# A new order of steps in the opening and at the passage into the loop of an attention and FFN kernel

## The chip, the cores and the metric

The kernel runs on one core of a Trainium2 chip. The metric is the device time of one execution in microseconds (us), the median of several runs. The engines are PE (TensorE, matmuls), DVE (VectorE), ACT (ScalarE), POOL (GpSimd) and SP, which only issues transfers. Each engine works through its own instructions in program order and waits for the others by semaphores.

## The reference

```python
# q, k, v: (8, 8, 576, 64): batch, heads, sequence, head size
k_p = k.reshape(B, H, 72, 8, D).mean(axis=3)          # 8 neighbours pooled: 72 keys
v_p = v.reshape(B, H, 72, 8, D).mean(axis=3)
attn = softmax(q @ k_p.T / sqrt(D)); x = attn @ v_p    # -> x: (8, 576, 512)
xn = (x - mean) / sqrt(var + 1e-6) * g_ln              # per token
out = x + relu(xn @ w_ch1) @ w_ch2                     # 512 -> 2048 -> 512
```

## The kernel before

There are 36 tiles of 128 tokens, in nine chunks c of four tiles. For exactness in float32 each large matmul is three float16 matmuls on high and low parts. Chunks 0 and 1 use the weights as they are; from chunk 2 on the two FFN matmuls go by a scheme of seven products of half-sized blocks in place of eight (as Strassen's), for which sums of blocks of W1 and W2 are made on the way.

The kernel's work is written as small generators, named steps. Each `yield` ends a part. Two strings, START (chunks 0 and 1 and all preparation) and STEADY (the loop over chunks 2 to 8, with what is left of chunk 2's weights and of its second matmul), list step names; `run` goes through a string and advances the named step by one part. So the order of names is the program order on every engine, written out by hand; nothing reorders it except at the seam between the two strings, where the first parts of STEADY that are ready are moved forward. A name's n-th occurrence is its n-th part: the issue of matmuls is one part, the evacuation of their result on ACT or DVE another.

The steps that the text names:

- HK.b.i, HV.b.i: half of the keys or values of batch b: an SP load into one of two buffers (kr, vr), then pooling of 8 neighbours on POOL (L647 to L673) or DVE (L651, L668). HK fills the block kblk, HV ends with a maximum and a split into high and low parts; D spreads the values to their places by DMA.
- A.t: scores of tile t: matmuls (L787), maximum and subtraction on DVE (L797, L802), exponential on ACT, the low part on POOL (L823), and a transposing DMA on SP's queue (L834). B.t: attention values (L926, L927), then scaling and statistics on DVE (L934 to L955), z on POOL or DVE.
- R, C, S, M1, M2: raw weight load, conversion and maximum (C: L523 a maximum, L539 a conversion, both DVE), split into high and low (L486 on DVE), and the scale from the maximum (M1, M2: L558, L559, L443, L444 on DVE around one PE transpose L466).
- F.c.f: one tile of the first FFN matmul, 12 matmuls (L1110), relu on ACT (L1119), low part on DVE (L1121). In chunk 0 a third index takes half the columns. G.c.tt.half: half of the second FFN matmul of tile tt, 24 matmuls of 512 columns (L1313), then one DVE instruction that adds it to x (L1324).
- P.c.h.f.m: one of the seven products m, 6 matmuls of 256 columns (L1154), then an ACT copy (L1173) or a DVE addition (L1168, L1171). WH joins the products of an f into the hidden tile (L1184). TW: sums of W2's blocks (DVE L1233, POOL L1238 to L1246). TS.c: token scales of a chunk, a chain of DVE instructions on 128x4 elements (L1028 to L1059). EL, ER, ES, EP: left factors of the second matmul's products.

What couples them are buffers. PSUM in the opening: one buffer for A, one for B, three for F and G, one for the rest. In the loop: one for A and B together, six for P and G; the products 1, 6 and 7 of a block share a bank, so do 2 and 4, and 5 and 3, and each such bank is used again only after its evacuation. A step's matmuls that need a bank stand on PE until the step that had it is evacuated.

Of the kernel before, what the change touches and what calls it, by code (L numbers as in the profile page):

```python
# [87 lines left out]
F.0.12 S.2.4 S.2.4 S.2.5 B.6 HV.2.1 HV.2.1 F.0.15 S.2.5 S.2.5 S.2.6 F.0.14 F.0.15 B.6 B.6 B.6 A.10 A.11 A.10 F.0.13
F.0.13 S.2.6 S.2.6 S.2.7 HV.2.1 HV.2.1 F.0.14 F.0.14 F.0.15 F.0.15 S.2.7 S.2.7 G.0.0.1 G.0.1.1 G.0.2.1 HV.2.1 HV.2.1
HV.2.1 HV.2.1 B.7 B.7 A.10 HV.3.0 HV.3.0 HV.3.0 HV.3.0 G.0.0.1 T.1.0 T.1.0 B.7 HV.3.0 HK.3.0 HK.3.0 G.0.0.1 G.0.0.1  # L90
HV.3.0 A.10 A.10 HV.3.1 B.7 B.7 G.0.1.1 G.0.1.1 G.0.1.1 HV.3.0 HV.3.0 B.8 B.9 G.0.3.1 A.11 A.11 G.0.2.1 HV.3.1 HV.3.1
HK.3.1 G.0.2.1 G.0.2.1 B.9 V.10 F.1.0 F.1.1 F.1.0 A.11 HV.3.1 HV.3.1 A.11 A.11 G.0.3.1 F.1.2 T.1.0 HV.3.1 HV.3.1
# [1367 lines left out]
```

## Time and profile before

| | us |
|---|---|
| median of 3 runs (lowest, highest) | 813.83 (812.39 to 814.22) |
| the profiled execution, its own time | 812.09 |
| its span, first to last instruction | 810.3 |
| PE busy in the span | 780.9 |
| DVE busy in the span | 666.6 |

The profile is of one execution. Its span is what the engines' rows cover; the execution's own time is 1.8 us longer. PE's busy time is 96% of the span, with the granted clock at its full level. Times in the rows are counted from the start of the span.

### The profile page before, as it was taken

Reading aid. Unit: us, or ns where it says so; the run is one execution under the profiler, and the core shown is the slowest. Engines: PE = TensorE matmul, PEld = TensorE weight load, DVE = VectorE, ACT = ScalarE, POOL = GpSimd, SP = SyncE. Lnnn points to the kernel's source line nnn. Section 1 sums busy time; section 2 is a strip of 40 time slices with the busy share of each in tenths; the row PEclk is TensorE's granted clock in tenths of the full one; section 3 lists DMA queues with packets and bytes.
Section 4 is the critical chain, followed back from the end, with each engine's and each line's share of the span. In section 5 each row is a group of like instructions: output and inputs, shape, how many; then the busy total and the mean of one; then the engine's idle time right before and its main releaser. Section 6 shows DMA issues by size and latency. Waiting matters only on the chain.

```text
span 810.3 us, 17383 instructions
## 1 busy us (share of the span) xinstructions
PE 780.9 (96%) x6618; PEld 608.3 (75%) x6618; DVE 666.6 (82%) x1352; ACT 470.5 (58%) x880; POOL 488.8 (60%) x601
## 2 busy tenths in 40 slices
...
GB/s 355 283 167 301 236 168 126 205 18 8 45 114 121 181 208 132 199 187 243 199 176 177 222 188 238 131 260 161 233 99 209 162 131 167 169 153 161 77 120 130
DMA packets 181507, 138.91 MB, mean 171 GB/s; under 512 B 143792, under 2 KB 151600, under 8 KB 179248
## 3 DMA queue, kind: packets, MB, share of 16 engines
...
## 4 chain that ended last, share of the span: by engine, by line
PE 55%; DVE 6%; ACT 1%; issue 1%; DVEq 0%; ACTq 0%
PE ps_f L1271 25%; PE ps_f L1154 25%; PE ps_a L787 2%; DVE w L1192 1%; PE ps_f L1313 1%; PE ps_a L926 1%; PE ps_a L927 1%; DVE ring L1184 1%; DVE x L1288 0%; DVE phl L1168 0%; DVE raw L1168 0%; DVE mx L797 0%; DVE raw L1012 0%; DVE raw L1013 0%; DVE y L1043 0%
## 5 line engine op out<-in xcount | busy, mean ns | idle before, releaser
L1271 PE MATMUL ps_f<-ring,w 128*128 128x256 f16 x2016 | 231.3, 273 | 1.3 <-DVE w L1192 1.0
L1271 PEld LDWEIGHTS <-w 128*128 128x128 f16 x2016 | 196.6, 98 | 25.2 <-DVE w L1192 1.5
L1154 PE MATMUL ps_f<-zts,w 128*128 128x256 f16 x1680 | 206.8, 273 | 2.5 <-DVE x L1324 1.2
L1154 PEld LDWEIGHTS <-w 128*128 128x128 f16 x1680 | 163.5, 98 | 23.4 <-issue 3.9
L1313 PE MATMUL ps_f<-w,ring 128*128 128x512 f16 x576 | 126.4, 379 | 2.3 <-DVE x L1324 2.2
L1173 ACT COPY raw<-ps_f 128x256 f32<-128x256 f32 x160 | 56.3, 372 | 91.4 <-PE ps_f L1154 80.7
L1313 PEld LDWEIGHTS <-ring 128*128 128x128 f16 x576 | 56.1, 98 | 68.3 <-issue 2.6
L1154 PE MATMUL ps_f<-zts,tsp 128*128 128x256 f16 x672 | 91.0, 272 | 1.7 <-ACT raw L1173 1.7
L1110 PE MATMUL ps_f<-zts,w 128*128 128x512 f16 (+1 forms) x480 | 85.9, 336 | 2.5 <-DVE ring L1121 0.9
L1190 ACT CAST w<-w 128x512 f16<-128x512 f32 x96 | 59.0, 618 | 44.1 <-POOL w L1210 21.5
L1192 POOL TENSOR_TENSOR w<-w 128x512 f16<-128x512 f32 x48 | 58.4, 1216 | 32.1 <-ACT w L1190 22.6
L1110 PEld LDWEIGHTS <-w 128*128 128x128 f16 x480 | 46.4, 98 | 39.0 <-issue 3.3
L1154 PEld LDWEIGHTS <-tsp 128*128 128x128 f16 x672 | 65.0, 98 | 10.1 <-issue 2.3
L823 POOL TENSOR_TENSOR phl<-e,phl 128x512 f16<-128x512 f32 x32 | 40.9, 1278 | 45.6 <-ACT phl L813 45.6
L1209 POOL TENSOR_TENSOR w<-raw 128x256 f32<-128x256 f32 x32 | 24.8, 775 | 65.8 <-ACT raw L1201 38.1
L1288 DVE SCALAR_TENSOR_TENSOR x<-ps_f,y,x 128x256 f32<-128x256 f32 (+1 forms) x84 | 42.0, 517 | 23.7 <-PE ps_f L1271 22.5
L1079 POOL TENSOR_TENSOR hl<-raw,hl 128x640 f16<-128x640 f32 x28 | 40.9, 1463 | 24.9 <-ACT hl L1077 24.7
L1288 DVE SCALAR_TENSOR_TENSOR x<-ps_f,cy,x 128x256 f32<-128x256 f32 (+1 forms) x84 | 42.1, 516 | 13.1 <-PE ps_f L1271 12.5
L1192 DVE TENSOR_TENSOR w<-raw,w 128x512 f16<-128x512 f32 (+1 forms) x64 | 44.9, 708 | 3.9 <-ACT w L1190 3.8
L1168 DVE TENSOR_TENSOR raw<-ps_f,raw 128x256 f32<-128x256 f32 x80 | 32.2, 415 | 15.7 <-ACT raw L1173 9.2
L787 PE MATMUL ps_a<-kblk,q 128*128 128x144 f32 (+1 forms) x320 | 42.0, 289 | 1.4 <-PE ps_f L1154 0.8
L1119 ACT ACTIVATE ring<-ps_f 128x512 f16<-128x512 f32 (+1 forms) x40 | 19.4, 506 | 38.4 <-PE ps_f L1110 38.4
...
## 6 DMA issues: line engine op xcount, KB each, us to landing
...
```

Of the source, the lines that this page charges most:

```text
L787: nc.tensor.matmul(ps[r, p // 2, p % 2 * 2 * KV : (p % 2 + 1) * 2 * KV], lhsT=q[:, p, r], rhs=kblk[b % NKB][:, p, :], start=True, stop=True,)
L823: nc.gpsimd.tensor_tensor(out=ph[:, 0, :, KA:P], in0=e[:, :, 0:KA], in1=ph[:, 0, :, 0:KA], op=ALU.subtract)
L1079: nc.gpsimd.tensor_tensor(out=zhl[:, 1, :], in0=src, in1=zhl[:, 0, :], op=ALU.subtract)
L1110: nc.tensor.matmul(ps, lhsT=w[:, part, fs], rhs=zT[:, kz, cols], start=(n == 0), stop=(n == 3 * NKT - 1),)
L1154: nc.tensor.matmul(ps, lhsT=w[:, part, f * P : (f + 1) * P], rhs=z, start=m in (1, 2, 4, 5) and n == 0, stop=m in (2, 3, 4, 7) and n == 3 ...
L1168: nc.vector.tensor_tensor(out=o, in0=ps, in1=o, op=ALU.add)
L1173: nc.scalar.copy(out=o, in_=ps)
L1190: nc.scalar.copy(out=hi, in_=src)
L1192: engine.tensor_tensor(out=lo, in0=src, in1=hi, op=ALU.subtract)
L1271: nc.tensor.matmul(ps, lhsT=wt[2][:, left, part, f * HC + u * P : f * HC + (u + 1) * P], rhs=b[:, f // FPB, wp, f % FPB], start=n < 4 and ...
L1288: nc.vector.scalar_tensor_tensor(out=x, in0=ps, scalar=scale, in1=x, op0=ALU.mult, op1=ALU.add)
L1313: nc.tensor.matmul(ps, lhsT=h[:, part, i, cols], rhs=w[:, wp, j], start=(n == 0), stop=(n == 3 * NFT // 2 - 1),)
```

## The change

Both strings get a new order in one stretch each: START from its sixth line to its end (60 to 160 us of the profile, on PE), and STEADY from its first step to about the first products of chunk 3's second half (240 to 375 us), and a handful of exchanges of neighbours later. No code changes: the same steps, the same number of instructions on each engine, the same buffers. The core of the diff, without the lines that the text does not speak of:

```diff
--- before.py
+++ after.py
@@ START @@
...
-F.0.5.1 A.6 C.1.5 C.1.5 S.2.1 F.0.3.1 F.0.4.1 A.6 C.1.6 S.2.1 S.2.1 S.2.2 F.0.5.1 F.0.3.1 F.0.3.1 F.0.4.1 F.0.4.1 C.1.4
-C.1.4 C.1.7 A.6 S.2.2 S.2.2 S.2.3 HK.2.0 HK.2.0 S.2.3 S.2.3 HV.2.0 HV.2.0 HK.2.1 A.7 A.7 F.0.6.1 B.4 F.0.7.1 F.0.6.1
-C.1.6 F.0.7.1 A.7 A.7 M1.1 F.0.5.1 F.0.5.1 B.4 C.1.4 C.1.4 C.1.5 C.1.5 F.0.6.1 F.0.6.1 C.1.6 C.1.6 HV.2.0 B.4 A.7
-HK.2.1 HK.2.1 R.2.4 R.2.4 A.6 A.6 HV.2.0 R.2.5 R.2.5 R.2.6 R.2.6 HK.2.1 HK.2.1 HV.2.0 HV.2.0 A.8 A.8 M1.1 G.0.0.0 B.5
-G.0.1.0 A.7 A.7 M1.1 M1.1 S.1.4 C.2.4 B.5 B.6 F.0.7.1 F.0.7.1 G.0.2.0 S.1.4 S.1.4 S.1.5 C.1.7 C.2.5 G.0.0.0 G.0.0.0
-G.0.3.0 S.1.5 S.1.5 S.1.6 B.4 C.1.7 C.1.7 R.2.7 R.2.7 HV.2.1 A.8 A.8 C.2.6 S.1.6 S.1.6 S.1.7 B.6 G.0.1.0 G.0.1.0 A.8
-B.4 HV.2.0 HV.2.0 B.5 HV.2.1 HV.2.1 A.8 A.8 HV.2.1 HV.2.1 A.9 B.4 B.4 HK.3.0 A.9 B.7 A.9 A.9 S.1.7 S.1.7 F.0.8 F.0.8
-C.2.7 G.0.2.0 G.0.2.0 C.2.4 C.2.4 C.2.4 B.5 G.0.3.0 G.0.3.0 C.2.5 C.2.5 C.2.5 C.2.6 C.2.6 C.2.6 F.0.8 F.0.8 C.2.7 B.7
-HV.2.1 HV.2.1 HV.3.0 B.5 B.5 B.5 HV.2.1 B.6 A.9 A.9 A.9 A.10 A.10 F.0.9 F.0.10 F.0.11 B.8 F.0.9 F.0.10 F.0.11 C.2.7
...
+HV.1.1 HV.1.1 D.1 D.1 R.1.7 R.1.7 B.4 HK.2.0 S.2.1 S.2.1 S.2.2 C.1.6 F.0.4.1 F.0.4.1 F.0.3.1 F.0.3.1 F.0.6.1 F.0.7.1
+F.0.7.1 F.0.5.1 A.6 B.4 S.2.2 S.2.2 S.2.3 F.0.6.1 A.7 C.1.5 F.0.5.1 F.0.5.1 B.4 B.4 C.1.5 C.1.7 C.1.7 S.2.3 S.2.3
+HV.2.0 HV.2.0 A.5 A.5 HK.2.0 A.6 A.6 HK.2.1 R.2.4 R.2.4 B.5 A.7 B.5 M1.1 F.0.6.1 F.0.6.1 C.1.5 C.1.5 F.0.7.1 F.0.7.1
+HK.2.0 HK.2.0 A.7 HK.2.1 HK.2.1 R.2.5 R.2.5 A.7 A.7 HK.2.1 HK.2.1 HV.2.0 HV.2.0 B.4 B.5 HV.2.0 HV.2.0 A.8 A.8 G.0.0.0
+B.6 M1.1 G.0.1.0 G.0.2.0 M1.1 M1.1 S.1.4 C.2.4 C.1.6 G.0.0.0 G.0.0.0 S.1.4 S.1.4 S.1.5 C.2.5 A.8 S.1.5 S.1.5 C.1.6
+C.1.6 S.1.6 R.2.6 R.2.6 C.1.7 C.1.7 R.2.7 R.2.7 B.4 B.4 HV.2.1 HK.3.0 S.1.6 S.1.6 S.1.7 A.8 B.5 C.2.6 G.0.1.0 G.0.1.0
+C.2.4 S.1.7 S.1.7 G.0.2.0 G.0.2.0 A.8 B.6 HV.2.0 HV.2.0 B.5 HV.2.1 HV.2.1 B.6 HV.2.1 HV.2.1 B.5 B.5 HV.2.1 HV.2.1 A.8
+A.8 HV.3.0 A.9 A.9 G.0.3.0 F.0.8 F.0.9 B.7 F.0.8 C.2.7 F.0.9 G.0.3.0 G.0.3.0 F.0.10 F.0.8 F.0.8 F.0.11 C.2.5 C.2.5
+C.2.5 F.0.10 C.2.6 C.2.6 C.2.6 C.2.7 C.2.7 C.2.7 C.2.4 C.2.4 F.0.11 F.0.9 F.0.9 F.0.12 F.0.12 A.9 A.9 F.0.10 F.0.10
+M2.1 HK.3.0 A.9 A.9 A.9 A.10 A.10 M2.1 F.0.13 M2.1 M2.1 S.2.4 F.0.11 F.0.11 F.0.14 F.0.12 F.0.12 F.0.15 S.2.4 S.2.4
+S.2.5 F.0.14 F.0.13 B.6 HV.2.1 B.7 B.8 S.2.5 S.2.5 S.2.6 F.0.15 B.6 HV.2.1 HV.2.1 F.0.13 F.0.13 S.2.6 S.2.6 S.2.7
...
@@ STEADY @@
-P.2.0.0.2 P.2.0.0.1 P.2.0.0.5 P.2.0.1.2 P.2.0.0.1 P.2.0.0.1 P.2.0.0.6 P.2.0.1.1 P.2.0.1.1 P.2.0.1.1 P.2.0.0.5 P.2.0.0.5
-P.2.0.0.6 P.2.0.0.6 HV.4.0 KW.1.1 KW.1.1 A.12 A.12 P.2.0.1.6 TW.0.0.0 TW.0.0.0 P.2.0.0.2 P.2.0.0.2 P.2.0.0.4 P.2.0.1.5
-P.2.0.0.7 P.2.0.0.3 TW.0.0.0 TW.0.0.0 P.2.0.1.6 P.2.0.1.6 P.2.0.1.7 TW.0.0.1 TW.0.0.1 TW.0.0.1 TW.0.0.1 P.2.0.0.4
-P.2.0.0.4 TW.0.0.0 A.12 A.12 HV.4.0 HV.4.0 TW.0.0.0 TW.0.0.0 TW.0.0.1 P.2.0.1.2 P.2.0.1.2 P.2.0.1.4 P.2.0.2.2 P.2.0.1.4
-P.2.0.1.4 P.2.0.1.5 P.2.0.1.5 P.2.0.0.7 P.2.0.0.7 P.2.0.3.1 P.2.0.1.3 TW.0.1.0 A.12 P.2.0.0.3 P.2.0.0.3 P.2.0.3.5
-P.2.0.2.1 WH.2.0.0 TW.0.1.0 TW.0.1.1 P.2.0.1.7 P.2.0.1.7 TW.0.1.0 WH.2.0.0 WH.2.0.0 TW.0.1.1 P.2.0.1.3 P.2.0.1.3
...
-P.2.1.3.6 P.2.1.3.6 P.2.1.2.2 P.2.1.2.2 P.2.1.2.4 B.15 A.16 P.2.1.2.7 P.2.1.3.7 TS.3 B.15 HV.4.1 HV.4.1 TW.1.0.0 Z.14.0
-Z.14.0 TW.1.0.1 TW.1.0.0 TW.1.0.0 P.2.1.2.4 P.2.1.2.4 Z.14.1 Z.14.1 TW.1.0.1 TW.1.0.1 TW.1.0.0 P.2.1.3.3 P.2.1.3.3
-P.2.1.3.2 P.2.1.3.2 P.2.1.3.4 P.2.1.3.4 P.2.1.3.4 P.2.1.2.3 P.2.1.2.3 TW.1.0.1 A.16 P.2.1.2.7 P.2.1.2.7 WH.2.1.2 B.15
-P.2.1.3.7 P.2.1.3.7 WH.2.1.3 A.16 WH.2.1.2 WH.2.1.2 TW.1.1.0 TW.1.1.0 TS.3 WH.2.1.3 WH.2.1.3 A.16 B.15 B.15 TW.1.1.0
-TS.3 TW.1.1.1 TS.3 TS.3 TS.3 HV.5.0 HV.5.0 KW.1.0 KW.1.0 TW.1.0.0 TW.1.0.0 A.17 KW.0.1 KW.0.1 XT.14.0 XT.14.0 XT.14.1
-XT.14.1 TW.1.0.1 TW.1.0.1 A.16 A.16 A.17 G.2.0.1 P.3.0.1.2 P.3.0.0.2 G.2.3.1 P.3.0.0.1 P.3.0.1.1 TW.1.1.0 Z.15.0 HV.4.1
-HV.4.1 Z.15.1 P.3.0.1.1 P.3.0.1.1 P.3.0.0.1 P.3.0.0.1 TW.1.1.0 Z.15.0 Z.15.0 TW.1.1.1 Z.15.1 Z.15.1 HV.5.0 HV.5.0
-XT.15.0 XT.15.0 TW.1.1.0 TW.1.1.0 G.2.0.1 G.2.2.1 G.2.0.1 G.2.0.1 TW.1.1.1 TW.1.1.1 P.3.0.0.2 P.3.0.0.2 TW.1.2.0
-TW.1.2.0 A.17 A.17 P.3.0.1.2 P.3.0.1.2 P.3.0.1.4 B.16 P.3.0.0.4 TW.1.2.0 TW.1.2.0 P.3.0.1.4 P.3.0.1.4 G.2.1.1 TW.1.1.1
-TW.1.2.1 TW.1.2.1 G.2.2.1 A.17 TW.1.2.0 TW.1.2.1 TW.1.3.0 TW.1.3.0 TW.1.3.0 B.16 HV.5.0 HV.5.0 TW.1.1.1 TW.1.1.1
...
+P.2.0.1.2 P.2.0.0.1 P.2.0.1.1 P.2.0.1.1 P.2.0.1.1 HV.4.0 KW.1.1 KW.1.1 A.12 A.12 P.2.0.0.2 P.2.0.0.5 P.2.0.0.1
+P.2.0.0.1 TW.0.0.0 TW.0.0.1 TW.0.0.1 A.12 TW.0.0.1 TW.0.0.1 P.2.0.0.5 P.2.0.0.5 TW.0.0.0 P.2.0.1.2 P.2.0.1.2 P.2.0.1.4
+P.2.0.0.6 P.2.0.0.3 P.2.0.1.6 TW.0.0.0 TW.0.0.0 P.2.0.0.6 P.2.0.0.6 A.12 P.2.0.1.6 P.2.0.1.6 P.2.0.1.4 P.2.0.1.4 HV.4.0
+HV.4.0 TW.0.0.1 TW.0.0.0 TW.0.0.0 TW.0.0.0 P.2.0.0.3 P.2.0.0.3 HV.4.0 HV.4.0 A.13 TW.0.1.0 P.2.0.0.2 P.2.0.0.2
+P.2.0.0.4 P.2.0.1.5 P.2.0.0.7 P.2.0.1.7 P.2.0.0.4 P.2.0.0.4 P.2.0.1.5 P.2.0.1.5 P.2.0.1.3 P.2.0.3.2 A.12 A.12 A.12
+TW.0.1.1 P.2.0.0.7 P.2.0.0.7 P.2.0.3.1 WH.2.0.0 TW.0.1.0 P.2.0.1.7 P.2.0.1.7 P.2.0.2.2 A.13 P.2.0.3.5 P.2.0.2.1
...
+P.2.1.2.4 A.16 B.15 B.15 P.2.1.2.6 P.2.1.2.6 P.2.1.2.4 P.2.1.2.4 P.2.1.3.5 P.2.1.3.5 P.2.1.3.2 P.2.1.3.2 P.2.1.3.4
+P.2.1.2.7 P.2.1.3.3 P.2.1.3.4 P.2.1.3.4 TW.1.0.1 B.15 B.15 TW.1.1.0 P.2.1.2.3 P.2.1.2.3 P.3.0.0.2 P.2.1.2.7 P.2.1.2.7
+WH.2.1.2 TW.1.1.0 P.2.1.3.7 P.2.1.3.7 P.2.1.3.3 P.2.1.3.3 WH.2.1.3 TW.1.0.1 A.16 TW.1.0.1 WH.2.1.2 WH.2.1.2 WH.2.1.3
+WH.2.1.3 G.2.3.1 TS.3 TS.3 TS.3 TS.3 TS.3 TS.3 HV.5.0 HV.5.0 KW.1.0 KW.1.0 TW.1.0.0 TW.1.0.0 A.17 KW.0.1 KW.0.1 XT.14.0
+XT.14.0 XT.14.1 XT.14.1 A.17 G.2.0.1 P.3.0.0.1 P.3.0.1.2 G.2.2.1 Z.15.0 TW.1.0.1 Z.15.1 A.16 Z.15.0 Z.15.0 TW.1.1.0
+TW.1.1.0 TW.1.0.1 TW.1.0.1 TW.1.0.1 A.16 A.16 A.16 TW.1.1.0 Z.15.1 Z.15.1 TW.1.1.1 TW.1.1.1 G.2.0.1 TW.1.1.1 TW.1.1.1
+P.3.0.0.1 P.3.0.0.1 TW.1.2.0 HV.5.0 HV.5.0 XT.15.0 XT.15.0 TW.1.1.0 TW.1.1.0 G.2.0.1 G.2.0.1 TW.1.2.0 TW.1.1.1 A.17
+A.17 P.3.0.0.2 P.3.0.0.2 P.3.0.0.4 B.16 P.3.0.0.4 P.3.0.0.4 TW.1.2.0 TW.1.2.0 TW.1.2.1 G.2.3.1 TW.1.2.1 HV.5.0 HV.5.0
+TW.1.1.1 TW.1.1.1 XT.15.1 XT.15.1 P.3.0.0.6 P.3.0.1.1 P.3.0.0.5 P.3.0.0.6 P.3.0.0.6 P.3.0.1.1 P.3.0.1.1 P.3.0.0.7
+P.3.0.1.6 P.3.0.1.6 P.3.0.1.6 A.17 TW.1.2.0 TW.1.2.0 TW.1.2.0 A.18 A.17 A.17 B.16 P.3.0.1.2 P.3.0.1.2 P.3.0.1.4 G.2.1.1
...
```

In the opening the scores A.6, A.7 and A.9 and the values B.4 to B.6 come earlier among the F and G steps, the conversions C.1.4 earlier and C.1.7 later, M1.1 behind G.0.0.0, A.10 and B.8 later. In the passage the products begin in another order, TS.3 goes in one piece behind WH.2.1.3 and G.2.3.1, and the four second halves of G.2 come in the order 3, 0, 2, 1 instead of 0, 3, 2, 1.

## Rows read from the trace of the kernel before

**Rows 1.** The page's span, and the busy time of each engine: us, share of the span, instructions.

```profile
span 810.3 us, 17383 instructions
...
PE 780.9 (96%) x6618; PEld 608.3 (75%) x6618; DVE 666.6 (82%) x1352; ACT 470.5 (58%) x880; POOL 488.8 (60%) x601
```

**Rows 2.** Busy time of each engine by stretches: stretch, its length, then us busy (and instructions) on each engine, PE's granted clock, the share of the DMA engines that was busy, GB/s.

```profile
60.00:150.00 90.00, 84.11 (x558) 47.87 (x557) 82.48 (x156) 63.33 (x88) 69.05 (x83) 1.00 0.77 211
150.00:240.00 90.00, 89.16 (x443) 40.94 (x442) 67.33 (x115) 23.89 (x42) 41.51 (x39) 1.00 0.24 64
240.00:285.00 45.00, 43.67 (x400) 34.44 (x399) 40.24 (x80) 25.82 (x55) 29.92 (x44) 1.00 0.67 146
285.00:325.00 40.00, 36.40 (x240) 22.68 (x239) 38.19 (x91) 18.77 (x35) 23.46 (x33) 1.00 0.74 168
325.00:340.00 15.00, 14.56 (x98) 8.53 (x98) 10.46 (x22) 4.92 (x10) 12.15 (x20) 1.00 0.89 196
340.00:380.00 40.00, 40.00 (x390) 36.12 (x389) 36.23 (x79) 29.60 (x60) 30.33 (x39) 1.00 0.82 221
```

**Rows 3.** PE's timeline in the opening: start, duration, what ran and how often without a break, and in brackets the idle time ahead of it and what ended it.

```profile
74.66 1.47 PE L1110 MATMUL ps_f<-zts,w 128*128 128x256 f16 x12 [0.61 <-DVE ring L1121]
...
81.54 0.23 PE L466 MATMUL ps_m<-ident,rowmax 128*128 128x128 bf16 x1 [1.51 <-DVE rowmax L444]
81.87 5.34 PE L1313 MATMUL ps_f<-w,ring 128*128 128x512 f16 x24
...
87.73 5.34 PE L1313 MATMUL ps_f<-w,ring 128*128 128x512 f16 x24
...
107.28 2.54 PE L1110 MATMUL ps_f<-zts,w 128*128 128x512 f16 x11 [0.81 <-DVE x L1324]
110.51 0.39 PE L1110 MATMUL ps_f<-zts,w 128*128 128x512 f16 x1 [0.70 <-DVE w L486]
...
120.48 1.89 PE L1110 MATMUL ps_f<-zts,w 128*128 128x512 f16 x8 [0.31 <-DVE ring L1121]
```

**Rows 4.** PE's timeline in the passage, the same columns.

```profile
239.60 2.78 PE L1154 MATMUL ps_f<-zts,w 128*128 128x256 f16 x24 [0.84 <-DVE x L1324]
...
255.52 0.49 PE L1154 MATMUL ps_f<-zts,tsp 128*128 128x256 f16 x3 [1.09 <-ACT raw L1173]
...
309.01 1.22 PE L787 MATMUL ps_a<-kblk,q 128*128 128x144 f32 x8 [0.81 <-PE ps_f L1154]
310.07 5.34 PE L1313 MATMUL ps_f<-w,ring 128*128 128x512 f16 x24
315.25 1.47 PE L1154 MATMUL ps_f<-zts,w 128*128 128x256 f16 x12
316.56 5.34 PE L1313 MATMUL ps_f<-w,ring 128*128 128x512 f16 x24
...
325.44 5.34 PE L1313 MATMUL ps_f<-w,ring 128*128 128x512 f16 x24 [2.22 <-DVE x L1324]
...
337.62 0.49 PE L1154 MATMUL ps_f<-zts,tsp 128*128 128x256 f16 x3
```

**Rows 5.** DVE's timeline in the opening, the same columns.

```profile
78.63 1.33 DVE L558 TENSOR_SCALAR wm<-wm 128x4 f32<-128x4 f32 x1
...
89.61 0.21 DVE L934 TENSOR_SCALAR sm<-ps_a,cv 128x8 f32<-128x8 f32 x1
...
91.65 0.39 DVE L1121 SCALAR_TENSOR_TENSOR ring<-ps_f,ring 128x256 f16<-128x256 f32 x1
...
119.77 0.66 DVE L1121 SCALAR_TENSOR_TENSOR ring<-ps_f,ring 128x512 f16<-128x512 f32 x1
```

**Rows 6.** DVE's groups in 60 to 100 us by line and shape: count, busy us, mean ns of one, idle time ahead.

```profile
L523 DVE TENSOR_REDUCE wm<-raw 128x1 f32<-128x1024 f32 x2 | 2.4, 1212 | 0.0
...
L802 DVE TENSOR_TENSOR e<-ps_a,mx 128x576 f32<-128x576 f32 x3 | 2.3, 758 | 0.3
L797 DVE TENSOR_REDUCE mx<-ps_a 128x8 f32<-128x576 f32 x3 | 2.2, 745 | 0.0
...
L539 DVE SCALAR_TENSOR_TENSOR w<-w,tsp 128x1024 int32<-128x1024 int32 x1 | 1.2, 1208 | 0.0
```

**Rows 7.** POOL's timeline in the opening, and one row of it at 346 us.

```profile
77.79 2.15 POOL L483 TENSOR_TENSOR w<-w 128x1024 f16<-128x1024 f32 x1 [1.09 <-ACT w L481]
...
84.55 1.71 POOL L671 TENSOR_TENSOR vr<-vr 72x256 f32<-72x256 f32 x1
...
87.73 1.25 POOL L673 TENSOR_TENSOR vp<-vr 72x64 f32<-72x64 f32 x1
...
98.23 0.72 POOL L655 TENSOR_TENSOR kblk<-kr 64x72 f32<-64x72 f32 x2
...
346.16 1.61 POOL L1246 TENSOR_TENSOR phl<-kr,phl 128x512 f16<-128x512 f32 x1
```

**Rows 8.** DVE's timeline in the passage.

```profile
241.56 0.42 DVE L1168 TENSOR_TENSOR raw<-ps_f,raw 128x256 f32<-128x256 f32 x1 [2.01 <-ACT raw L1173]
...
253.74 0.67 DVE L668 TENSOR_REDUCE vp<-vr 72x64 f32<-72x512 f32 x1
...
318.43 1.11 DVE L1042 TENSOR_TENSOR a<-a,ve 128x4 f32<-128x4 f32 x1
...
324.63 0.75 DVE L1324 SCALAR_TENSOR_TENSOR x<-ps_f,cy,x 128x512 f32<-128x512 f32 x1
```

216 lines of the change are left out of this document (107 added, 109 removed).

## The prediction, made before the changed kernel ran

> **What bounds the kernel now.** I read the busy shares first: PE 780.9 of 810.3 us, DVE 666.6 [rows 1]. PE's clock is 1.00 in every stretch [rows 2], so the matmuls themselves can't get shorter; a new order can only change PE's idle time. The windows say where that lies [rows 2]: 5.89 us of it in 60 to 150, 0.84 in 150 to 240, 1.33 in 240 to 285, 3.60 in 285 to 325, 0.44 in 325 to 340, none in 340 to 380. The change reaches 61 to 160 and 240 to 375, nearly the same places.
>
> PE's timeline names the waits. In the opening there are 0.61 on an evacuation (L1121), 1.51 on the row maximum of W1's second half (L444), 0.81 ahead of F.0.8 (L1324) and 0.70 inside it (L486), 0.31 at F.0.12 [rows 3]. In the passage there are 1.09 on an ACT copy, 0.81 ahead of A.17's scores, 2.22 ahead of G.2.2.1 [rows 4]. Most of them are DVE being late, and DVE is busy for 82.48 of 90 us in the opening and 38.19 of 40 in 285 to 325 [rows 2]: there it is a second bound, close under PE.
>
> The idle column understates a wait. The 24 matmuls of a G step take 5.18 us from start to start (310.07 to 315.25), 0.216 each, and the 12 of two P steps 1.31 (315.25 to 316.56), 0.655 a P step [rows 4]; a lone matmul ahead of a change of step is drawn with 0.39 [rows 3], so a wait costs its idle time and about 0.16. With 5.89 + 5.37 us of idle time and some 15 waits the ceiling of any gain is near 13.7 us; the waits that stay or come new take most of it.
>
> **The change part by part.** No instruction is added, removed or resized. All costs are positions.
>
> *Opening, up to G.0.1.0.* G.0.0.0 needs the bank of F.0.5.1, so it starts when DVE has evacuated that: 81.87 now [rows 3]. Ahead of that evacuation DVE loses a maximum of W1 (C.1.7, 1.21 [rows 6]) and M1.1's chain, from 78.63 [rows 5] to the transpose at 81.54 [rows 3], 2.8 us, and gains B.4's finish (as B.5's, 89.61 to 91.65, 2.04 [rows 5]) and one C.1.4 conversion (1.21 as L539 [rows 6]). Net 0.8 less, and none to 0.7 of small waits besides: I take 0.9, G.0.0.0 at 81.0. B.5's matmuls (0.68, 87.05 to 87.73 [rows 3], the first by G's 5.18) are already done by then, where before they stand behind G.0.0.0. The 1.51 wait is not merely moved: M1.1's transpose now stands behind G.0.0.0 and B.6, by when DVE has long passed the row maximum. G.0.1.0 then starts near 81.0 + 5.18 + 0.68 (B.6) = 86.9, with B.6 done, against 87.73 with B.6 and a wait (0.9 together) to come: 1.7 gained.
>
> *Opening, G.0.2.0 to F.0.12.* After two G steps PE reaches A.9 at 97.3; A.9 needs A.8's maximum and subtraction done (0.4 wait, from DVE's new order) and the K block from POOL. A step of scores takes 1.06 (309.01 to 310.07 [rows 4]), so G.0.3.0 ends at 103.9. F.0.8 no longer follows B.7, and the weights it waits for (L486) stand two places earlier on DVE: the 0.81 and 0.70 go. PE alone would start F.0.12 at 103.9 + 4 x 2.59 (12 matmuls of 0.216 each) + 0.68 = 114.9. DVE allows less: F.0.12 needs F.0.9's evacuation, which starts at 119.77 [rows 5], less A.9's maximum and subtraction (0.75 + 0.76 [rows 6]) and B.7's finish (2.04), which now come behind it: 116.2, or down to 114.2 if DVE's own small waits go too. F.0.12 thus starts between 114.9 and 116.9. Before, it starts at 120.48 [rows 3] with A.10 (1.0) and B.8 (0.7) done that now come later, so the like time is 118.8. Gain 1.9 to 3.9.
>
> The 3.5 us of DVE work pushed behind F.0.9 must be hidden later. Cover: DVE has 7.5 us free in 60 to 150 and 22.7 in 150 to 240, where PE is almost full [rows 2]. Without that cover all 3.5 would come back, at A.10 and B.8. I take 3.3 for the opening (the 0.31 at F.0.12 and the waits after it can go too); ends 1.5 and 5.2. POOL and SP: HK.2.0's second half goes behind HV.2.0's 4.4 us of pooling (84.55 to 88.98 [rows 7]), which frees a K buffer at about 91 instead of 82. Behind the load that waits for it, SP's queue has R.2.5, the transpose of A.7, loads of V and the last raw weights, which land some 7 us later than before; their readers (C.2.6, C.2.7) stand ahead of F.0.9's evacuation, 13 us on. Cost nothing; were they 1 us late, 1 us.
>
> 150 to 240 is full on PE with DVE at 67.33 of 90 [rows 2]: a gain of the opening arrives at 239.6 whole.
>
> *Passage, early part.* PE's P steps begin in the order 0.1.2, 0.0.1, 0.1.1, A.12 instead of 0.0.2, 0.0.1, 0.0.5, 0.1.2 (all of chunk 2). This makes two new waits. P.2.0.1.4 uses the bank of P.2.0.1.2, whose evacuation DVE issues behind A.12's 1.5 us: A.12's scores end at 239.6 + 3 x 0.655 + 1.0 = 242.6, the evacuation 2 us later, PE is there at 243.9: 0.8. P.2.0.0.4 uses that of P.2.0.0.2, now evacuated behind P.2.0.0.3, a reduction of V (0.67) and a sum of W2 of like size, six places later, where it was the first of all at 241.56 [rows 8]: PE is there at 247.3, the evacuation is done at 248.9: 1.6. Further 0 to 0.8 at G.2.3.0, and 0.5 in small waits. The 1.09 at 255.52 [rows 4] goes. G.2.0.0 starts 1 to 2.1 us later than before.
>
> *Passage, late part.* G.2.2.1 waits 2.22 us [rows 4] for the bank of G.2.0.1, whose evacuation stands on DVE behind TS.3, token scales of 128x4 elements with 1.11 us on a single instruction, and starts at 324.63 [rows 8]. In the new order the first step of TS.3 comes eleven places later, G.2.3.1 and G.2.0.1 are exchanged, A.17 comes behind the first of them, and G.2.2.1's bank is one that P steps have long freed. All idle time of 285 to 340 (4.04 [rows 2], four waits, 4.7 us with 0.16 each) can go; one of 0.45 comes at P.3.0.0.2. Followed through PE's new order from the later G.2.0.0, G.2.1.1 ends at 337.35 to 338.5, against 337.62 [rows 4], with four more P steps (2.62) done: 1.75 to 2.9 gained. I take 1.8; ends 0.5 and 3.
>
> *A rule against it.* Row first: L558 works on four columns and takes 1.33 us, to 79.96 [rows 5]; POOL's instruction begun at 77.79 ends at 79.94 [rows 7]; an evacuation of 512 columns takes 0.75 [rows 8]. The Trainium skill (SBUF — State Buffer, Who interferes with whom) says that VectorE and GpSimd share a port pair that one of them holds for a whole instruction, while the other is fully blocked, if the VectorE instruction has two SBUF inputs or a 2-port mode; the trace agrees in that row. By it, work packed closer meets POOL more often, and the sum could come out at nothing; without it, at -5.1.
>
> **Sum.** -3.3 - 1.8 = -5.1 on the profiled execution's 812.09: 807.0. The median of the runs, 813.83, stands 1.74 above that execution: 808.7.
>
> **Rivals.**
> (a) The passage's gain is given back after 340. POOL's sum of W2 at 346.16 [rows 7] and the splits around it follow work that DVE now does at other times, while PE has no idle time until 380 [rows 2]; buffers of the left factors come free only with them. For it: four more P steps ask for these buffers sooner. Against: the first of them lie some 5 us on. Time: 813.83 - 3.3 = 810.5.
> (b) DVE remains the bound in both places: it is busy for 92% and 95% there [rows 2], and its instructions grow where POOL meets them. Each meeting like L558's costs 0.58 (1.33 against the 0.75 of 512 columns) to 1.33; four to eight more take back most of the 5.1. Against: M1.1 and TS.3, which lose most now, move to places less pressed. Time: 812.3 to 815.4, no change.
> (c) All waits named go, with the upper ends: -5.2 - 3 = -8.2, 805.6, and down to 803.2 if the two new waits of the passage (2.4) don't come.
> (d) Slower. A.9 now stands ahead of G.0.3.0 and needs the K block that POOL makes last. POOL's order to it is HV.2.0, HK.2.0, A.7, both halves of HK.2.1; it ends near 96.6, where it ended at 98.95 before [rows 7], and PE wants it at 97.3. Each us over 0.7 that POOL or the K load is late goes to PE in full. L671 takes 1.71 us at 84.55; lateness of 5.8 us cancels the whole gain and 7.4 us puts it 0.2% above. For it: the load waits for a buffer that is freed 9 us later. Against: POOL has lost one 2-us step that stood ahead. Time at 8 us: 816.0.
>
> **How the numbers follow.** The measurement can tell 0.2% (1.6 us) from no change, so faster means below 812.2, slower above 815.5. Chances: the sum 0.44, (a) 0.18, (c) 0.14, so faster 0.76; (b) 0.14; (d) 0.10. The sum's own range goes from 811.8 (the lower ends, -1.5 - 0.5) to 806.3 (-7.5, short of both upper ends). The range 804.8 to 813.0 takes in the sum, (a), most of (c) and a part of (b), about 8 in 10.
>
> **What would show it.** Right: no wait of 1.5 us ahead of M1.1's transpose; G.0.0.0 at 80.3 to 81.3; F.0.8 without a wait on L486; two new waits of 0.8 and 1.6 in the first 10 us of the passage; none of 2.2 ahead of G.2.2.1; PE full after 340. Wrong if: A.9's scores wait over a us for POOL; F.0.12 waits longer than 0.3 for DVE; idle time on PE appears after 340; or DVE's time in 60 to 150 grows above 84.

## The result and the profile after

The changed kernel is slower: 817.92 us median (815.98 to 819.13 in 5 runs) against 813.83 (812.38 to 814.22), a ratio of 1.0056 with a 95% interval of 1.0042 to 1.0070. The forecast was 808.7, range 804.8 to 813.0. The profiled execution took 818.58 us, its span is 816.8, 6.5 more than before [rows 1], where the medians are 4.1 apart. All ratios here leave out executions that were disturbed and ran several per cent longer or more.

The page's span and busy times of the changed kernel:

```profile
span 816.8 us, 17391 instructions
...
PE 785.4 (96%) x6618; PEld 610.9 (75%) x6618; DVE 661.9 (81%) x1352; ACT 470.1 (58%) x880; POOL 486.6 (60%) x601
```

PE is busy 4.5 us longer with the same 6618 matmuls, DVE 4.7 us less. The windows of the changed kernel (columns as in rows 2) say where:

```profile
60.00:150.00 90.00, 85.01 (x560) 49.53 (x560) 78.81 (x158) 66.08 (x92) 66.55 (x82) 0.98 0.78 212
...
285.00:325.00 40.00, 39.07 (x252) 23.68 (x251) 37.71 (x88) 15.39 (x29) 22.42 (x31) 1.00 0.77 180
325.00:340.00 15.00, 10.84 (x73) 7.10 (x71) 7.97 (x17) 4.74 (x11) 9.72 (x18) 0.77 0.84 191
340.00:380.00 40.00, 40.00 (x367) 33.82 (x365) 34.88 (x73) 26.72 (x55) 31.16 (x42) 1.00 0.69 201
```

In 285 to 325 PE's idle time went from 3.60 to 0.93, as wanted. In 325 to 340 it rose from 0.44 to 4.16, and the granted clock, 1.00 there before [rows 2], is 0.77. In the opening the clock is 0.98. PE's timeline of the changed kernel, opening (columns as in rows 3):

```profile
81.87 0.20 PE L926 MATMUL ps_a<-va,pt 128*128 128x65 f16 x1 [2.37 <-DMA pt<-phl]
...
82.40 1.64 PE L787 MATMUL ps_a<-kblk,q 128*128 128x144 f32 x8
83.84 6.65 PE L1313 MATMUL ps_f<-w,ring 128*128 128x512 f16 x24
...
144.10 0.19 PE L926 MATMUL ps_a<-va,pt 128*128 128x65 f16 x1 [1.32 <-issue]
```

and in the passage:

```profile
240.07 2.12 PE L1154 MATMUL ps_f<-zts,w 128*128 128x256 f16 x18 [0.84 <-DVE x L1324]
...
245.15 0.82 PE L1154 MATMUL ps_f<-zts,w 128*128 128x256 f16 x6 [0.66 <-DVE raw L1168]
...
249.45 1.47 PE L1154 MATMUL ps_f<-zts,w 128*128 128x256 f16 x12 [1.52 <-DVE raw L1168]
...
322.68 5.34 PE L1313 MATMUL ps_f<-w,ring 128*128 128x512 f16 x24
...
333.39 0.80 PE L1154 MATMUL ps_f<-zts,tsp 128*128 128x256 f16 x3 [4.16 <-DMA zts<-hl]
333.98 3.40 PE L1154 MATMUL ps_f<-zts,w 128*128 128x256 f16 x15
```

The waits that were to go are gone: none of 1.51 at M1.1, none at F.0.8 or F.0.12, none of 2.22 ahead of G.2.2.1 (322.68). In their place stand three that no step of the prediction named. B.5 (81.87) waits for A.5's transpose, P.3.0.0.6 (333.39) for the transpose of XT.15.1, and B.9 (144.10) behind B.8, which is held up on DVE. SP's queue, which issues those transfers, in the changed kernel (start, duration, line and transfer):

```profile
71.48 0.48 SPq L761 DMA_DIRECT2D va<-vh  x1
...
74.03 0.44 SPq L506 DMA_DIRECT2D tsp<-in_w_dram  x1
...
74.94 4.81 SPq L834 DMA_TRANSPOSE pt<-phl  x1
...
130.18 10.54 SPq L1084 DMA_TRANSPOSE zts<-hl  x2
140.81 0.55 SPq L1329 DMA_DIRECT2D out_dram<-x  x1
...
329.43 1.36 SPq L1070 DMA_TRANSPOSE zts<-hl  x1
```

and three rows of it in the kernel before:

```profile
63.46 0.85 SPq L506 DMA_DIRECT2D tsp<-in_w_dram  x2
...
74.70 2.94 SPq L834 DMA_TRANSPOSE pt<-phl  x1
...
329.85 1.27 SPq L1070 DMA_TRANSPOSE zts<-hl  x1
```

The two transposes leave SP when they did before (74.94 against 74.70, 329.43 against 329.85). Their readers do not: B.5 ran at 87.05 [rows 3] and was now due at 79.50 (81.87 - 2.37); the products that read XT.15.1 ran at 337.62 [rows 4] and were due at 329.2. A.5's transpose also takes longer: R.1.7's load of 1 MB, the second of the two at 63.46 before, now stands right ahead of it (74.03). Third, the output of G.0.0.1 stands on SP behind the transposes of B.6 and B.7, of which the second had its data only at 139.5. DVE's timeline of the changed kernel shows what that holds up:

```profile
143.31 0.69 DVE L944 TENSOR_TENSOR x<-ps_a,rs 128x512 f32<-128x512 f32 x1 [3.18 <-DMA out_dram<-x]
```

B.8 writes the x buffer that this output reads, and PE's B.9 needs the one PSUM buffer of B, which this instruction of B.8 frees (the profile names no releaser for B.9; this is read from the code and the times).

Each of the two long waits is followed by matmuls at half pace. Windows of 2 us of the changed kernel (columns as in rows 2; the third from the end is the granted clock):

```profile
80.00:82.00 2.00, 0.13 (x4) 0.13 (x5) 1.90 (x3) 1.35 (x2) 1.90 (x3) 1.00 1.18 252
...
84.00:86.00 2.00, 2.00 (x7) 0.63 (x5) 1.86 (x6) 2.00 (x3) 2.00 (x2) 0.50 0.80 190
...
330.00:332.00 2.00, 0.00 (x0) 0.00 (x0) 1.93 (x5) 0.14 (x1) 1.92 (x5) 1.00 1.07 202
332.00:334.00 2.00, 0.61 (x4) 0.45 (x5) 0.99 (x3) 0.00 (x0) 1.92 (x4) 0.56 0.62 139
334.00:336.00 2.00, 2.00 (x11) 1.40 (x10) 0.00 (x0) 0.37 (x1) 0.17 (x1) 0.50 0.83 196
```

0.50 is 1.2 GHz in place of 2.4. The account: at B.5 2.37 and 0.16 of wait, A.8 takes 1.44 from start to start (82.40 to 83.84) instead of 0.98, and G.0.0.0 6.49 to the next step at 90.33 instead of 5.18, together 4.3 us. At P.3.0.0.6 4.33 (B.16's first matmul at 328.55 and 0.51 for its sixteen make 329.06) and 2.7 of slow products (worked out under the mended passage below), 7.1 us. With B.9's 1.3 that is 12.7 us. The span grew by 6.5, but 0.7 of it is there where the two orders are still the same (the matmul of L727 that starts at 12.14 before starts at 12.86 here). So in this pair of executions the change costs 5.8, and the rest of it gained 6.9, where the sum had said 5.1. This is an account, not a measurement: no run has the rest without the waits. At the first products of the passage the changed kernel is 0.47 behind (240.07 against 239.60 [rows 4]), so the opening, its two waits included, had gained some 0.2, and the loss lies behind it.

### The profile page after: what moved, and what is told of

The parts are those of the page before. It is cut to its first block, busy times and chain, and to the rows that moved or that the text cites. A ratio compares the mean times of both kernels' runs of the same rounds, so it can differ in the third digit from the quotient of the medians.

```text
span 816.8 us, 17391 instructions
## 1 busy us (share of the span) xinstructions
PE 785.4 (96%) x6618; PEld 610.9 (75%) x6618; DVE 661.9 (81%) x1352; ACT 470.1 (58%) x880; POOL 486.6 (60%) x601
## 4 chain that ended last, share of the span: by engine, by line
PE 75%; DVE 14%; DMA 5%; ACT 2%; issue 2%; POOL 2%; SPq 1%; DVEq 0%; POOLq 0%
PE ps_f L1154 27%; PE ps_f L1271 24%; PE ps_f L1313 11%; PE ps_f L1110 7%; PE ps_a L787 3%; DMA pt<-phl 2%; DVE w L486 2%; DVE w L539 1%; DVE w L1192 1%; DMA zts<-hl 1%; PE ps_a L926 1%; PE ps_m L727 1%; PE ps_a L927 1%; DVE x L944 1%; DVE mx L797 1%
## 5 line engine op out<-in xcount | busy, mean ns | idle before, releaser
L1313 PE MATMUL ps_f<-w,ring 128*128 128x512 f16 x576 | 128.2, 382 | 0.8 <-DVE w L486 0.4
L1173 ACT COPY raw<-ps_f 128x256 f32<-128x256 f32 x160 | 56.3, 372 | 93.6 <-PE ps_f L1154 86.7
L823 POOL TENSOR_TENSOR phl<-e,phl 128x512 f16<-128x512 f32 x32 | 38.6, 1207 | 32.2 <-ACT phl L813 32.0
L787 PEld LDWEIGHTS ps_a<-kblk,q 128*128 128x128 f32 (+1 forms) x320 | 37.8, 181 | 2.6 <-issue 1.4
```

The costliest lines, as they stand in the source:

```text
L787: nc.tensor.matmul(ps[r, p // 2, p % 2 * 2 * KV : (p % 2 + 1) * 2 * KV], lhsT=q[:, p, r], rhs=kblk[b % NKB][:, p, :], start=True, stop=True,)
L823: nc.gpsimd.tensor_tensor(out=ph[:, 0, :, KA:P], in0=e[:, :, 0:KA], in1=ph[:, 0, :, 0:KA], op=ALU.subtract)
L1173: nc.scalar.copy(out=o, in_=ps)
L1313: nc.tensor.matmul(ps, lhsT=h[:, part, i, cols], rhs=w[:, wp, j], start=(n == 0), stop=(n == 3 * NFT // 2 - 1),)
```

## Experiments

All kernels compute the whole output; in each only names in the two strings move. Ratios are against the kernel before, measured in the same sitting, with 95% intervals; medians in us. Two changed kernels are compared by these ratios, across sittings.

**Halves.** The new START with the old STEADY, and the other way round.

> The new START with the old STEADY: the opening's half of the change alone. Theory (two transposing DMAs on SP that PE now reaches too early, each followed by a stretch at the lower clock): in the opening the new order gains about what I forecast, and the wait of B.5 for A.5's transpose (2.5 us) and the lower clock behind it (1.8 us) give it back; counted from the first scores the changed kernel stood 0.15 us ahead at G.0.3.1 and 0.25 at the seam. So 813.6 us, between 812.8 and 814.4, PE's clock below 1.00 once, near 84 us, and the 2.4 us wait there. Rival (DVE stays the bound, longer instructions against POOL): the same time, but no wait of PE on a transposing DMA and the waits on DVE still there. Rival (the whole loss is the opening's): 817 to 818.

Measured: 812.99 against 812.92, 1.0006 (0.9991 to 1.0020).

> The old START with the new STEADY: the passage's half alone. Theory: it carries the whole loss. PE reaches P.3.0.0.6 some 7 us early, waits 4.8 us for XT.15.1's transposing DMA, and runs the next five P steps at half clock (2.7 us more); the early waits of 0.7 and 1.5 us are there too. 817.5 to 820 us, clock below 1.00 once, near 334 us. Rival (the loss needs both halves, as the seam arrives at another time): under 815.

Measured: 816.54, 1.0054 (1.0034 to 1.0074), a little under what was expected, with 2.95 of wait for XT.15.1 and a clock of 0.83 in 320 to 340. The passage carries the loss; the opening gives its own gain back.

**XT earlier on SP.** The changed kernel with the two transposes right behind the steps that make their data:

```diff
-Z.15.0 Z.15.0 TW.1.1.0 ... Z.15.1 Z.15.1 TW.1.1.1 ... HV.5.0 XT.15.0 XT.15.0 ... TW.1.1.1 XT.15.1 XT.15.1
+Z.15.0 Z.15.0 XT.15.0 TW.1.1.0 ... Z.15.1 Z.15.1 XT.15.1 TW.1.1.1 ... HV.5.0 XT.15.0 ... TW.1.1.1 XT.15.1
```

> The changed kernel with two names moved: the transposing DMAs XT.15.0 and XT.15.1 stand on SP's queue right behind the parts that they transpose (Z.15.0, Z.15.1), ahead of DMAs of W2's sums, a load of V and an output. Z.15.1 is ready at 324.2, its transpose was issued at 329.4. Theory: the wait at P.3.0.0.6 shrinks from 4.8 us to under 1.5 and the clock stays at 1.00 there (2.7 us): 5 to 7.5 us less than the changed kernel, 810.5 to 813. Rival (the transposes are late because DMA engines are full, at 0.97 to 1.24 of their time there, not because of SP's order): the transposes land only as late as before, less than 2 us gained. Rival (POOL's sums of W2 set the pace behind): the wait goes, and PE waits as long at P.3.0.0.3 to P.3.0.3.5.

Measured: 812.68, 0.9999 (0.9986 to 1.0012), in the range expected and 4.6 us below the changed kernel by the two ratios. With two names moved on SP's queue, the loss against the kernel before is gone. No trace of this kernel is read here; the same move was made in the old opening:

> The old START with the STEADY in which XT.15.0 and XT.15.1 stand right behind Z.15.0 and Z.15.1: the passage alone without its late transpose. Theory: 3.5 to 5 us less than the passage alone (816.5), 811.5 to 813, clock 1.00 throughout, since my forecast of the passage (1.8 less than before, 811.1) is met but for up to 1.5 us that is left of the wait at P.3.0.0.6. Rival (a): the gain is given back after 340, by waits on evacuations or on POOL's sums: then idle time of PE shows in 340 to 400 and the time is that of before, 813.

Measured: 811.59 against 812.24, 0.9994 (0.9985 to 1.0004). SP and PE of this kernel (its lines are three lower: L1151 is the products' line, L1067 the transpose's):

```profile
322.62 1.32 SPq L1067 DMA_TRANSPOSE zts<-hl  x1
```

```profile
238.58 2.13 PE L1151 MATMUL ps_f<-zts,w 128*128 128x256 f16 x18 [0.84 <-DVE x L1321]
...
327.57 0.49 PE L1151 MATMUL ps_f<-zts,tsp 128*128 128x256 f16 x3
327.90 1.82 PE L1151 MATMUL ps_f<-zts,w 128*128 128x256 f16 x15
...
330.54 0.49 PE L1151 MATMUL ps_f<-zts,w 128*128 128x256 f16 x3
...
384.63 0.81 PE L1151 MATMUL ps_f<-zts,w 128*128 128x256 f16 x6 [0.65 <-ACT raw L1170]
```

The transpose leaves SP 6.8 us sooner, no product waits for it, and the 27 matmuls from 327.57 to 330.54 take 2.97; the changed kernel's take 5.70 (333.39 to 339.09), which gives the 2.7 above. At the last steps before the wait at 384.63 PE is 2.56 us ahead of the kernel before (the same steps begun, each counted from its span's start), behind that wait 1.75. But 1.02 of this was there when the passage began, with the START the same in both (238.58 against 239.60 [rows 4]). So the passage gained 1.5, and the wait gave back 0.8 of it. The forecast for the passage was 1.8; by the ratio it is 0.5, with an interval that ends at 1.2.

**Filling the wait on PE instead.** G.2.1.1's matmuls go ahead of P.3.0.0.6.

```diff
-XT.15.1 XT.15.1 P.3.0.0.6 ... P.3.0.1.4 G.2.1.1 TW.1.2.1
+XT.15.1 XT.15.1 G.2.1.1 P.3.0.0.6 ... P.3.0.1.4 TW.1.2.1
```

> The changed kernel with one name moved: the 24 matmuls of G.2.1.1 stand on PE ahead of P.3.0.0.6, the first that needs XT.15.1's transpose, as they did before the change. Theory (the transposing DMA is late because PE comes sooner, and the lower clock follows from the wait): PE fills the 4.8 us with these 5.2 us of work, the clock stays at 1.00, and 5 to 7.5 us of the changed kernel's time go: 810.5 to 813, the same as with the transposes moved up on SP. Rival (another thing behind it, sums of W2 on POOL or the evacuations, sets the pace): 814 or more, with as long a wait at another P step.

Measured: 817.46, 1.0069 (1.0053 to 1.0085): a miss. The transpose is no longer waited for and the clock stays at 1.00 there, but other waits stand behind, here on PE's timeline:

```profile
340.45 1.54 PE L1151 MATMUL ps_f<-zts,w 128*128 128x256 f16 x12 [0.59 <-ACT raw L1170]
343.36 0.81 PE L1151 MATMUL ps_f<-zts,w 128*128 128x256 f16 x6 [1.37 <-DVE x L1321]
```

That the products which G covered for are now late themselves, and that what needs their evacuations waits for them, is a reading of these rows; no run tests it.

**A.5's transpose ahead of D.1.** In the opening of the changed kernel SP waits 5.3 us for V's high part (to 71.48, above) with A.5's transpose behind D.1, though A.5's data were complete on POOL at 67.93.

```diff
-HV.1.1 HV.1.1 D.1 D.1 R.1.7 ... HV.2.0 HV.2.0 A.5 A.5
+HV.1.1 HV.1.1 A.5 D.1 D.1 R.1.7 ... HV.2.0 HV.2.0 A.5
```

> The changed kernel with one name moved: the transposing DMA of A.5 (its sixth part) stands on SP's queue ahead of D.1's four DMAs instead of eight issues behind them. A.5's low part is ready at 67.9, while SP stood until 71.5 at D.1. Theory: the transpose is issued near 68 instead of 74.9, B.5 no longer waits (2.5 us) and the clock stays at 1.00 (1.8 us); D.1's DMAs come up to 1.5 us later, which B.4 pays. 2 to 4 us less than the changed kernel: 814 to 816. Rival (DVE is the bound of the opening): within 0.5 us of the changed kernel, as PE then waits for DVE at F.0.12 instead.

Measured: 819.25, 1.0087 (1.0061 to 1.0112): a miss. SP and PE of this kernel (lines three lower):

```profile
69.24 7.03 SPq L831 DMA_TRANSPOSE pt<-phl  x1
76.37 0.53 SPq L758 DMA_DIRECT2D va<-vh  x1
```

```profile
79.67 0.19 PE L923 MATMUL ps_a<-va,pt 128*64 128x65 f16 x1 [3.44 <-DMA va<-vh]
```

The transpose holds SP for 7.03 us, D.1 comes 4.9 later, and B.4 waits 3.44 for V. The wait moved and grew.

**B.5 and B.6 later, weights earlier.** B.5's matmuls behind G.0.0.0, B.6's behind G.0.1.0, R.1.5 to R.1.7 ahead; old STEADY, then with the mended passage.

```diff
-A.4 A.4 A.6 R.1.5 R.1.5 HV.2.0 R.1.6 R.1.6 ... D.1 D.1 R.1.7 R.1.7
+A.4 A.4 R.1.5 R.1.6 R.1.7 A.6 R.1.5 HV.2.0 R.1.6 ... D.1 D.1 R.1.7
-B.5 A.7 B.5 M1.1 ... HV.2.0 B.4 B.5 HV.2.0 HV.2.0 A.8 A.8 G.0.0.0 B.6 M1.1 G.0.1.0 G.0.2.0
+A.7 M1.1 ... HV.2.0 B.4 HV.2.0 HV.2.0 A.8 A.8 G.0.0.0 B.5 B.5 B.5 M1.1 G.0.1.0 B.6 G.0.2.0
```

> The old STEADY and the new START with these names moved: the raw weight loads R.1.5, R.1.6, R.1.7 ahead of the loads of q and V, as before the change (in the changed kernel C.1.6's maximum on DVE waits 1.4 us for R.1.6, and with it the evacuations behind it), and B.5's first three parts behind G.0.0.0, B.6's matmuls behind G.0.1.0, so that PE does not come to A.5's transpose too early. Theory (SP's order is what took the opening's gain): G.0.0.0 starts 1 to 2 us earlier than in the changed kernel, the 2.4 to 3.0 us wait of B.5 and the lower clock are gone, and 2 to 4 us of what I forecast for the opening appear: 809 to 811. Rival (DVE is the bound there whatever SP does): 812.4 to 813.5, waits of PE on DVE ahead of A.8 or G.0.0.0 instead.

Measured: 814.58, 1.0033 (1.0023 to 1.0044): a miss. PE's timeline:

```profile
77.05 0.19 PE L923 MATMUL ps_a<-va,pt 128*64 128x65 f16 x1 [1.67 <-DMA va<-vh]
...
81.58 1.22 PE L784 MATMUL ps_a<-kblk,q 128*128 128x144 f32 x8 [1.05 <-issue]
...
324.75 7.03 PE L1310 MATMUL ps_f<-w,ring 128*128 128x512 f16 x24 [2.23 <-DVE x L1321]
```

B.5 no longer waits, but B.4 does, for D.1, and A.8 after it. A.5's transpose, with no weight load near ahead of it, takes 1.71 us of SP:

```profile
76.08 1.71 SPq L831 DMA_TRANSPOSE pt<-phl  x1
```

> The START of the run before (loads of weights early, B.5 and B.6 back behind G steps) with the new STEADY in which XT.15.0 and XT.15.1 stand right behind Z.15.0 and Z.15.1 on SP. Theory: both gains add up, since 150 to 240 us is full on PE: the opening's 2 to 4 us and the passage's 0 to 2: 807.5 to 811. Rival (the gains do not add, as the seam comes at another time): no less than the better of the two alone.

Measured: 814.35, 1.0025 (1.0013 to 1.0036): a miss, B.4's wait now 2.69.

**G.0.0.1's output earlier on SP.** Ahead of the transposes of B.6 and B.7, in the new opening, with the old STEADY:

```diff
-B.7 HV.3.0 HV.3.0 B.6 B.6 G.0.0.1 G.0.0.1 HK.3.0
+B.7 HV.3.0 HV.3.0 G.0.0.1 B.6 B.6 G.0.0.1 HK.3.0
```

> The new START, in which one name is moved, with the old STEADY. The output DMA of G.0.0.1 stands on SP ahead of the transposes of B.6's and B.7's z instead of behind them. In the changed kernel B.8's x takes the buffer that this output empties; the output's DMA, ready at 137.8, is issued at 140.8 behind a transpose that waits for POOL, B.8's DVE part waits 3.2 us for it, and PE waits 1.3 us at B.9 for B.8. Theory: B.9's wait goes, 1.0 to 1.5 us less than the opening alone: 811.4 to 812.2. Rival (that wait has another cause, the profile names none): unchanged, 813.

Measured: 811.42 against 812.82, 0.9983 (0.9971 to 0.9995), as expected. SP, and DVE's B.8:

```profile
137.30 0.35 SPq L1329 DMA_DIRECT2D out_dram<-x  x1
137.74 2.65 SPq L1084 DMA_TRANSPOSE zts<-hl  x2
```

```profile
139.64 0.69 DVE L944 TENSOR_TENSOR x<-ps_a,rs 128x512 f32<-128x512 f32 x1
```

B.8 goes without the 3.18, and B.9 doesn't wait. Against the new opening without this move the ratio falls by 0.0023, 1.9 us.

**The new orders from a later point on.** The old opening up to G.0.2.0, then the new one with the output moved; the old STEADY up to G.2.2.0, then the new one with XT moved; and both.

> The START in which only the late part of the opening has the new order: the old order up to G.0.2.0, and from there what is left in the new order, with the output DMA of G.0.0.1 moved as in the run before; the old STEADY. Theory: the new order's loss lies ahead of G.0.2.0 (SP: weights, D.1, A.5's transpose), its gain behind it: from G.0.2.0 to G.0.0.1 the changed kernel won 2.8 us on the kernel before. So 1.5 to 3 us less than before: 809.3 to 811. Rival (that gain only made up for what was lost ahead, since DVE is the bound over the whole stretch): 812 to 813, with waits of PE on DVE at F.0.8 to F.0.12.

Measured: 811.60, 0.9987 (0.9975 to 0.9999), short of what was expected; A.9 waits 0.90 on DVE's L802.

> The old START, and the STEADY in which only the late part of the passage has the new order: the old order up to G.2.2.0, then what is left in the new one, with XT.15.0 and XT.15.1 moved up as in the passage's mended run. Theory: the two new waits of the early part (0.7 and 1.5 us, as forecast) are gone, and the late part's gain of 3.6 us (from G.2.2.0 to P.3.0.1.5 in the mended run) less 0.8 given back by 386 stays: 2 to 3.5 us less than before, 808.7 to 810.3. Rival (the late gain only makes up for the early waits): 811.5 to 812.5.

Measured: 812.64, 0.9998 (0.9983 to 1.0012): a miss. The two early waits of the passage are gone, and B.15 waits 2.06 for a transpose (L834) at 291.74 instead.

> The START and the STEADY of the two runs before, together. Theory (the gains add up): 3.5 to 6 us less than before, 806.5 to 808.8. Rival (they do not): as the better of the two.

Measured: 810.78 and 811.65, too few for a ratio: no verdict, though both lie above the range expected.

**The changed kernel with three names moved on SP.** G.0.0.1's output and the two XT, as above.

> The new START with the output DMA of G.0.0.1 moved up and the new STEADY with XT.15.0 and XT.15.1 moved up: the changed kernel but for three names on SP's queue. Theory (SP's order at these places is what turned the change from a gain into a loss, and 150 to 240 us carries the opening's gain): 1.4 less than before from the one and 0.7 from the other, 2.1 together: 810.2 to 811.2 where before is 812.6, and 5 to 7 less than the changed kernel. Rival (the halves do not add): as the opening's alone, 1.0 to 1.4 less, or nothing.

Measured: 810.74 against 812.18, 0.9984 (0.9973 to 0.9995), as expected. The step from 1.0056 to 0.9984, 5.9 us, is three transfers issued earlier. B.5's wait is still there (3.03), with a clock of 0.91 in 80 to 100.

**V earlier on DVE.** A.6's and C.1.4's DVE work goes behind V's maximum, so that D.1 and A.5's transpose leave SP sooner; START as with the output moved, first with the old STEADY, then with the mended passage.

```diff
-S.2.0 S.2.0 A.6 F.0.0.1 F.0.0.1 F.0.3.1 A.7 HV.1.1 ... A.6 C.1.4 C.1.4 F.0.2.1 F.0.2.1 F.0.5.1 HV.1.1
+S.2.0 S.2.0 F.0.0.1 F.0.0.1 F.0.3.1 A.7 HV.1.1 A.6 ... A.6 F.0.2.1 F.0.2.1 F.0.5.1 HV.1.1 C.1.4 C.1.4
```

> The new START with the output DMA of G.0.0.1 moved up as before, and on DVE the last two parts of V's preparation (HV.1.1) ahead of A.6's maximum and of C.1.4's conversion; the old STEADY. D.1's DMAs on SP wait for these parts, and A.5's transpose stands behind D.1. Theory (DVE's new order holds V back by 3 us, SP then holds back A.5's transpose, and B.5 waits): D.1 is issued 1.5 us earlier and A.5's transpose with it, the waits of B.4 and B.5 (1.4 and 1.2 us in the run with the output alone moved) shrink by 1.5 us or more: 1 to 2 us less than that run, 809.4 to 810.5. Rival (the transpose takes its time from full DMA engines, not from its place in the queue): B.5 waits as long, no gain.

Measured: 810.97, 0.9981 (0.9972 to 0.9990). The time is a little short of what was expected, and the mechanism is a miss. ACT, SP and PE:

```profile
70.77 0.71 ACT L479 ACTIVATE vh<-vp,sv 72x512 f16<-72x512 f32 x1
```

```profile
71.53 0.48 SPq L761 DMA_DIRECT2D va<-vh  x1
...
74.99 4.85 SPq L834 DMA_TRANSPOSE pt<-phl  x1
```

```profile
81.97 0.20 PE L926 MATMUL ps_a<-va,pt 128*128 128x65 f16 x1 [2.99 <-DMA pt<-phl]
```

DVE had V's scale at 69.24 instead of 70.26, but ACT works through its own order and makes V's high part at 70.77, where it made it at 70.67 in the changed kernel. D.1 and the transpose did not move.

> The START of the run before with the new STEADY, XT.15.0 and XT.15.1 moved up. Theory: all of it together, 3 to 4.5 us less than before, 808.2 to 809.6; with it the forecast of the opening (3.3) and of the passage (1.8) would be nearly met, and SP's order is shown as the one step that failed. Rival: the sum stays above 810, as DVE takes back at F.0.12 or A.9 what B.5 no longer waits.

Measured: 810.46, 0.9981 (0.9972 to 0.9989), B.5 still waiting 3.01: a miss. It is the lowest median of the sitting, but its interval is that of the two kernels beside it, and the forecast of the opening and of the passage is not met.

## Why the prediction was wrong

**The step that failed** is the sentence on POOL and SP, which followed SP's queue for K, V and raw weights and put it at nothing. It never asked, of the steps pulled forward on PE, when the transfers that they read land and what the new order puts ahead of them. Two phrases of the sum hold the failure. The passage's "with four more P steps (2.62) done" moves products ahead of G.2.1.1, from 337.62 to 329.2, while XT.15.1 stays at 329.4 to 329.9. This could have been read from the trace of before. "B.5's matmuls ... are already done by then" moves them from 87.05 to 79.5. Here the trace of before shows no wait, only that the cover is spent: in it A.5's transpose landed at 78.96 (the trace's record of the landing), half a us before B.5 is now due. In the changed kernel it leaves SP at the same time and lands at 81.83, since it takes 4.81 us of SP instead of 2.94, with R.1.7's load now right ahead of it. A third place of the same kind is the output of G.0.0.1, which came behind transposes that wait for POOL.

That SP's order is the cause is shown for XT.15 and for the output by moving those names alone (0.9999 and 0.9983). For A.5's transpose it is seen in the traces only: three attempts to mend it moved or left the wait. The two kernels with R.1.5 to R.1.7 ahead did shorten the transpose, but there V came late. What would bring it earlier without holding V stays open; DVE's order of V's scale is not it, and neither ACT's order nor R.1.7's load alone was tried.

**The second step that failed** is "PE's clock is 1.00 in every stretch". It was taken to hold in the new order too: there the waits of 2.37 and 4.16 were each followed by 1.2 GHz, which added 1.8 and 2.7 us. It was also read from one execution. Of 97 others of the kernel before, 16 have a mean granted clock of 1.000 and the rest 0.995 to 0.999; in each sitting those at 1.000 are shorter, by 1.1 to 1.9 us in the mean, than those at 0.997 and below. So some half clock belongs to the kernel before as well, and the profiled pair shows more of a loss than the medians do.

**What held.** The two new waits of the passage were forecast as 0.8 and 1.6 and measured 0.66 and 1.52. All waits that were to go went. M1.1's chain, put at 2.8, is 2.91 by its rows (78.63 to 81.54), which changes nothing. G.0.0.0 starts at 83.84 instead of 81.0, by B.5's wait and the slow A.8 behind it. F.0.12, the third of the three FFN steps that start at 113.12, begins near 118.3, where 114.9 to 116.9 was forecast, with 4.3 lost on the way at B.5. PE is full in 340 to 380, as said. The sum's size is not shown: the account above gives 6.9 for the rest of the change where the sum had 5.1, but the best kernels measured lie 1.3 to 1.5 us below the kernel before, with B.5's wait still in them. The passage's 1.8 was too much in any case: 0.5 by the ratio, mostly for the reason in (a).

**The rivals.** (a), the gain given back after 340, appears as one wait of 0.65 at 392 (L1173), the idle time that was to show the forecast wrong. In the kernel with the mended passage it takes back 0.8 of the 1.5 that the passage gained, so (a) came true in about half. (b), DVE remaining the bound, is not borne out: its busy time fell from 82.48 to 78.81 in the opening. The row that it started from, L558's 1.33 [rows 5], reads so in the changed kernel, DVE and POOL:

```profile
85.92 0.20 DVE L558 TENSOR_SCALAR wm<-wm 128x4 f32<-128x4 f32 x1
```

```profile
85.36 0.73 POOL L671 TENSOR_TENSOR vr<-vr 72x256 f32<-72x256 f32 x1
```

L558 ends 0.02 to 0.03 behind POOL's instruction in both kernels (79.96 and 79.94 before, 86.12 and 86.09 here), but here POOL was nearly done when it came. At 24.78, where POOL runs nothing beside it, it takes 0.17, so the meeting before cost 1.16, within the 0.58 to 1.33 of (b). The rule of the Trainium skill (SBUF — State Buffer, Who interferes with whom), one of the two being blocked while the other holds the ports, agrees with both rows; that closer packing costs more by it did not come true, DVE as a whole lost less. (c), all waits named gone, came true in those waits; whether its time would have followed without the three transfers is not shown. (d), A.9 waiting for POOL's K block, was right in its sign and not in its place: POOL ended it at 95.96 (forecast 96.6), and A.9 ran at 101.27 without a wait.
